# Attention followed by a gated linear unit: the depthwise convolutions of two units on one full TensorE array, with a new order of work

## The chip, the cores and the metric

One core of one Trainium2 chip. The metric is the device time of a run in microseconds (us); profile spans, given beside it, run from the first to the last instruction of one profiled execution.

## The reference, cut to what matters

B = 8 batches, H = 12 heads, S = 448 positions, D = 64, model width 768, convolution width K = 5.

```python
scores = q @ k.T / sqrt(D);  scores = where(causal, scores, -1e9)   # per head
x = softmax(scores) @ v                  # heads put side by side: [B, S, 768]
gate = sigmoid(causal depthwise convolution of x along S, with conv_w[K, 768])
out = (gate * (x @ w_val)) @ w_out       # float32
```

## The kernel before

The work is cut into 24 **units**: unit `n` is batch `n // 3` and a group of four heads. Each unit has scores in two stages, exps on ScalarE, causal masks on GpSimd, attention, a normalization on VectorE and a convolution. A batch has three value products (`val`), and each pair of batches 14 output blocks (`project`). The casting DMAs (q, k, both weight matrices), the masks and the casts of v to bf16 are all written on GpSimd, which works through them in program order. v itself is loaded by SyncE.

The convolution multiplies with 32x32 diagonal matrices, so each matmul takes one tile of the array. One unit has eight tiles per tap:

```python
def conv(n):
    x = xs[n % 8]; g = n % NG
    for t in range(KW):
        for dh in range(2):
            for i in range(G):
                j = 2 * (i % 2) + dh
                r = slice(32 * i, 32 * (i + 1))
                nc.tensor.matmul(
                    out=av_ps[i // 2][32 * j:32 * (j + 1), 0:S], lhsT=cwd[r, 2 * g + dh, t], rhs=x[r, dh, t:t + S],
                    start=t == 0, stop=t == KW - 1, skip_group_check=True, tile_position=(32 * i, 32 * j))
    ...   # two tanh on ScalarE
```

The loop takes one unit at a time:

```python
for n in range(N + 1):
    load_v(n + 2)
    ...
    scores(n, 0); softmax_numerators(n, 0)          # exps, then masks
    ...                                             # n == 0: value weights
    attend(n - 1); normalize(n - 1)                 # denominators, attention product
    next_out(limit, z_ps); next_out(limit, den_ps)  # two output blocks, in some units three
    scores(n, 1); softmax_numerators(n, 1)
    conv(n - 1)
    transposes(n + 1)
    cast_v(n + 1)                                   # a unit ahead of its use
    load_qk(n + 3)
    ...                                             # val(b - 1, g, (den_ps, z_ps))
```

The softmax here doesn't subtract the row's maximum and nothing guards it: scores larger than these inputs give would overflow.

## Time and profile before

| | before |
|---|---|
| median of 4 runs | 239.17 us (237.81 to 241.24) |
| profile span | 238.6 us |
| TensorE busy | 211.0 us, 88% |
| mean granted clock | 0.986 |

The prediction below shows the stretches and the timeline. These are the rows of the profile's 40 slices of the span for the kernel before (each 6 us; tenths busy, and tenths of the full TensorE clock). In all lines of the profile PE is TensorE, PEld its weight loads, DVE VectorE, ACT ScalarE and POOL GpSimd; L12 is line 12 of the kernel, and a bracket gives the idle time before an instruction and what ended it:

```profile
PE   0297389988988999999999999999999999999893
PEclk9999859999999999999999999999999999999999
```

After the seventh slice TensorE is nearly full and its clock reads full. Before it there are holes, and the clock row dips in two slices.

### The profile page before, as it was taken

The page shows a single profiled execution, that of the slowest core. Times are in us where ns is not written, and L with a number is a line of the kernel's source. Part 1 is how long each engine was busy: PE and PEld are TensorE (multiplying, and loading weights), DVE is VectorE, ACT ScalarE, POOL GpSimd, SP SyncE. Part 2 cuts the span into 40 slices and gives each one's busy share as a digit, 9 for nine tenths or more (in the row PEclk, how much of TensorE's full clock was granted, in tenths as well). Part 3 has the DMA queues.
Part 4 walks back from the last instruction along what each step waited for, and adds up shares of the span by engine and source line. Part 5 has one row for each costly group of instructions (what it writes and reads, how often), then busy time and mean ns, then how long its engine had stood idle before and what let it go on. Part 6 is the DMA issues. An engine that isn't in the chain of part 4 may idle for free.

```text
span 238.6 us, 10214 instructions
## 1 busy us (share of the span) xinstructions
PE 211.0 (88%) x4518; PEld 117.1 (49%) x4518; DVE 138.1 (58%) x235; ACT 143.1 (60%) x201; POOL 110.7 (46%) x189
## 2 busy tenths in 40 slices
PE   0297389988988999999999999999999999999893
PEld 0154145554544555545554555555555555544462
DVE  3457466754776678657766776586678663622100
ACT  2367543488765677668676867776777677231241
POOL 7594795153746535733655365347534532100000
PEclk9999859999999999999999999999999999999999
DMA  6999999959795568787768876877797111111153
GB/s 124 225 192 161 191 217 206 176 145 213 152 203 111 103 147 163 156 189 166 145 152 209 180 121 162 235 154 155 184 191 140 41 69 69 69 65 70 69 201 132
DMA packets 59574, 36.07 MB, mean 151 GB/s; under 512 B 48261, under 2 KB 55941, under 8 KB 59530
## 3 DMA queue, kind: packets, MB, share of 16 engines
q0 software_dynamic: 10944, 13.38, 35.4%
q1 hardware_dynamic: 48586, 22.04, 35.0%
q8 instruction: 35, 0.57, 1.0%
q14 instruction: 9, 0.07, 0.1%
HBM read 37.76 MB, written 11.01 MB: 204 GB/s over the span
## 4 chain that ended last, share of the span: by engine, by line
PE 77%; DMA 9%; POOL 3%; DVE 3%; issue 3%; ACT 3%; SPq 0%; POOLq 0%; DVEq 0%
PE den_ps L230 11%; PE z_ps L230 10%; PE av_ps L214 9%; PE z_ps L248 9%; PE sc_ps L154 9%; PE av_ps L187 8%; DMA kb<-in_k_dram 7%; PE den_ps L248 7%; PE sc_ps L248 5%; PE den_ps L187 5%; PE av_ps L230 2%; ACT ob L250 2%; ACT pt L163 1%; DMA vf<-in_v_dram 1%; DVE x L200 1%
## 5 line engine op out<-in xcount | busy, mean ns | idle before, releaser
L163 ACT ACTIVATE pt<-sc_ps 128x1024 bf16<-128x1024 f32 x96 | 93.0, 1021 | 50.4 <-PE sc_ps L154 49.1
L173 POOL TENSOR_SCALAR_AFFINE_SELECT pt<-pt 128x512 bf16<-128x512 bf16 x48 | 29.6, 642 | 59.3 <-ACT pt L163 48.4
L154 PE MATMUL sc_ps<-qt,kt 32*128 32x448 bf16 (+3 forms) x768 | 35.0, 285 | 17.7 <-DVE kt L140 13.4
L248 PEld LDWEIGHTS <-gv 128*32 128x32 bf16 x1344 | 35.3, 97 | 20.1 <-issue 5.3
L230 PEld LDWEIGHTS <-wv 128*128 128x128 bf16 x288 | 26.4, 98 | 30.4 <-issue 8.1
L154 PEld LDWEIGHTS <-kt 32*128 32x128 bf16 x768 | 17.4, 96 | 41.9 <-DVE kt L140 14.7
L232 DVE SCALAR_TENSOR_TENSOR gv<-gate,den_ps 128x448 bf16<-128x448 f32 x22 | 13.7, 621 | 32.5 <-ACT gate L219 22.6
L214 PE MATMUL av_ps<-x,cwd 32*32 32x448 bf16 x960 | 29.8, 349 | 2.3 <-DVE x L200 2.2
L200 DVE TENSOR_TENSOR x<-av_ps,rb 128x448 bf16<-128x448 f32 x48 | 27.7, 620 | 3.1
L230 PE MATMUL den_ps<-x,wv 128*128 128x448 bf16 x132 | 28.8, 354 | 0.0
L230 PE MATMUL z_ps<-x,wv 128*128 128x448 bf16 x132 | 28.6, 352 | 0.0
L76 POOL CAST vb<-vf 128x1024 bf16<-128x1024 f32 x24 | 24.9, 1037 | 6.7 <-DMA vf<-in_v_dram 6.7
L248 PE MATMUL z_ps<-wo,gv 128*32 128x384 bf16 x576 | 27.6, 326 | 0.0
L167 POOL TENSOR_SCALAR_AFFINE_SELECT pt<-pt 128x512 bf16<-128x512 bf16 x24 | 15.4, 642 | 25.6 <-ACT pt L163 25.6
L194 DVE STREAM_TRANSPOSE dt<-den_ps 128x448 f32<-128x448 f32 x24 | 15.6, 650 | 19.9 <-PE den_ps L187 19.9
L140 DVE STREAM_TRANSPOSE qt<-qb 128x448 uint32<-128x448 uint32 x24 | 22.9, 952 | 7.0 <-DMA qb<-in_q_dram 7.0
L187 PE MATMUL av_ps<-pt,vb 128*32 128x448 bf16 (+3 forms) x768 | 26.7, 283 | 0.0
L219 ACT ACTIVATE gate<-av_ps 128x448 f32<-128x448 f32 x48 | 23.7, 555 | 1.1 <-PE av_ps L214 0.8
L140 DVE STREAM_TRANSPOSE kt<-kb 128x448 uint32<-128x448 uint32 x24 | 22.4, 934 | 2.5 <-DMA kb<-in_k_dram 2.5
L248 PE MATMUL den_ps<-wo,gv 128*32 128x384 bf16 x456 | 21.9, 326 | 0.0
L187 PEld LDWEIGHTS <-vb 128*32 128x32 bf16 x768 | 17.2, 101 | 6.0 <-issue 0.8
L250 ACT ACTIVATE ob<-z_ps 128x384 f32<-128x384 f32 x24 | 11.8, 491 | 13.3 <-PE z_ps L248 13.3
(36 smaller groups left out, 161.7 us busy)
## 6 DMA issues: line engine op xcount, KB each, us to landing
out_dram<-ob SPq DMA_DIRECT2D x28, 384.0 KB, 3.4
vf<-in_v_dram SPq DMA_DIRECT2D x72, 128.0 KB, 4.5
qb<-in_q_dram POOLq DMA_DIRECT2D x24, 224.0 KB, 3.9
kb<-in_k_dram POOLq DMA_DIRECT2D x24, 224.0 KB, 5.1
vf<-in_v_dram SPq DMA_DIRECT2D x24, 64.0 KB, 3.7
wv<-in_moe_w_val_dram POOLq DMA_DIRECT2D x6, 192.0 KB, 10.6
wo<-in_moe_w_out_dram POOLq DMA_DIRECT2D x6, 192.0 KB, 8.2
cwn<-in_moe_conv_w_dram SPq DMA_DIRECT2D x1, 15.0 KB
```

What stands on the lines that cost most here:

```text
L76: nc.gpsimd.tensor_copy(out=t, in_=vfs.pop(n))
L140: nc.vector.transpose(out=t.bitcast(U32).rearrange("p (b s) -> p s b", s=T), in_=qks.pop((name, n)).rearrange("p s d -> p (s d)").bitcast( ...
L154: nc.tensor.matmul(out=sc_ps[h // 2][:, h % 2, c0:c0 + nq], lhsT=kt[r, e, k0:k0 + 128], rhs=qt[r, e, q0:S], start=e == 0, stop=e == 1, ski ...
L163: nc.scalar.activation(out=pt[:, 2 * hp:2 * hp + 2, 512 * stage:512 * (stage + 1)], in_=sc_ps[hp], func=AF.Exp, scale=D ** -0.5)
L173: nc.gpsimd.affine_select(out=pt[:, :, c:c + 128], in_=pt[:, :, c:c + 128], compare_op=ALU.is_ge, fill=0.0, base=0, pattern=[[0, G], [1, 1 ...
L187: nc.tensor.matmul(out=o, lhsT=w, rhs=pt[:, h, col:col + nq], start=i == 0, stop=i == 3, skip_group_check=True, tile_position=(0, 32 * h))
L200: nc.vector.tensor_tensor(out=x[:, dh, 4:S + 4], in0=av_ps[dh][:, 0:S], in1=r, op=ALU.mult)
L214: nc.tensor.matmul(out=av_ps[i // 2][32 * j:32 * (j + 1), 0:S], lhsT=cwd[r, 2 * g + dh, t], rhs=x[r, dh, t:t + S], start=t == 0, stop=t == ...
L219: nc.scalar.activation(out=gate[:, e], in_=av_ps[e][:, 0:S], func=AF.Tanh, scale=0.5)
L230: nc.tensor.matmul(out=o[e][:, 0:S], lhsT=wv_sb[c][:, f:f + 128], rhs=xs[(NG * b + cg) % 8][:, ce, 4:S + 4], start=c == 0, stop=c == NE - ...
L248: nc.tensor.matmul(out=o[r, 0:384], lhsT=gvs[p][g][:, dh, 128 * m + 32 * j:128 * m + 32 * (j + 1)], rhs=wo_sb[c][:, f], start=c == 0, stop ...
L250: nc.scalar.activation(out=ob[:, f], in_=o[:, 0:384], func=AF.Copy, scale=0.5)
```

## The change

The intent is to have two units share the array. Their eight tiles each become sixteen, with the heads of one unit swapped in pairs so that its tiles fall where the other's do not. The convolution moves to the four score banks, the loop takes units in pairs, the start is written out by hand, and ten idle matmuls at the very beginning are to keep the clock up. A head swap needs its own copies of the value weights and of the convolution tiles, four versions instead of three.

```diff
-    def conv(n):
+    def conv(p, banks):
+        units = (2 * p, 2 * p + 1)
         for t in range(KW):
             for dh in range(2):
                 for i in range(G):
+                    for u, n in enumerate(units):
+                        j = 2 * ((i ^ swapped(n)) % 2) + dh
...
+    def prefetch(n):
+        transposes(n + 1)
+        cast_v(n)
+        load_qk(n + 4)
... the start, from unit 1's first scores (cut at both ends)
+    exps(1, 0, 2)
+    conv_tiles()
+    attend(0)
+    normalize(0)
+    load_v(3)
+    exps(1, 1, 2)
+    load_wv(1, 0)
+    load_wv(1, 1)
+    cast_v(1)
+    transposes(2)
+    exps(2, 0, 2)
+    load_wv(2, 0)
+    load_wv(2, 1)
+    attend(1)
...
+    for p in range(2, N // 2 + 1):
+        n = 2 * p
+        load_v(n + 1)
+        exps(n, 0)
+        attend(n - 1)
+        normalize(n - 1)
+        next_outs(1, [z_ps])
+        exps(n, 1)
+        next_val((den_ps, z_ps))
+        prefetch(n)
+        conv(p - 1, sc_banks)
+        next_val(av_ps)
         if n < N:
+            load_v(n + 2)
+            exps(n + 1, 0)
+            attend(n)
+            normalize(n)
+            next_outs(1, [z_ps])
+            exps(n + 1, 1)
+            prefetch(n + 1)
+            next_outs((3, 3, 2)[p % 3], (den_ps, z_ps))
+            if p == 2:
+                for c in range(NE):
+                    load_wo(c)
```

`exps` is the scores, exps and masks of one stage; its last argument splits the scores by heads. `load_wv(i, half)` issues two DMAs.

## The prediction

> **What bounds the kernel now.** I read the page's sums and slices first, then the busy time by stretches, then the timeline of one unit (one batch of four heads; there are 24 units), then the waits of the first 60 us.
>
> The stretches show where TensorE has no time left. Columns: stretch, its length, busy time of each engine, granted clock, DMA share, GB/s.
>
> ```profile
> 0.00:8.60 8.60, 0.00 (x1) 0.01 (x2) 3.10 (x17) 1.28 (x1) 4.66 (x16) 1.00 0.85 162
> 8.60:31.00 22.40, 14.29 (x282) 7.70 (x286) 12.97 (x20) 13.59 (x16) 17.59 (x29) 0.94 1.25 187
> 31.00:43.00 12.00, 11.83 (x153) 6.12 (x146) 7.11 (x12) 4.75 (x6) 7.82 (x13) 0.84 1.14 209
> ...
> 107.00:131.00 24.00, 24.00 (x556) 13.27 (x548) 16.97 (x28) 17.20 (x24) 12.82 (x22) 1.00 0.76 167
> ```
>
> From 83 to 203 us every stretch reads PE 24.00 of 24.00: TensorE is the bound there, and a microsecond taken out of its order of work is a microsecond of time, unless a wait replaces it. Before 31 us it is busy for 14.3 of 31 us, with DMA saturated.
>
> One unit in the steady part, TensorE alone (start, length to the modelled end, operation, count):
>
> ```profile
> 114.39 0.63 PE L154 MATMUL sc_ps<-qt,kt 32*128 32x448 bf16 x16
> 114.95 0.62 PE L187 MATMUL den_ps<-pt,ones 128*32 128x448 bf16 x16
> 115.40 1.05 PE L187 MATMUL av_ps<-pt,vb 128*32 128x448 bf16 x32
> 116.27 1.15 PE L248 MATMUL z_ps<-wo,gv 128*32 128x384 bf16 x24
> 117.25 1.15 PE L248 MATMUL den_ps<-wo,gv 128*32 128x384 bf16 x24
> 118.33 0.64 PE L154 MATMUL sc_ps<-qt,kt 32*128 32x320 bf16 x16
> 118.90 1.14 PE L214 MATMUL av_ps<-x,cwd 32*32 32x448 bf16 x40
> 119.97 1.31 PE L230 MATMUL den_ps<-x,wv 128*128 128x448 bf16 x6
> 121.11 1.30 PE L230 MATMUL z_ps<-x,wv 128*128 128x448 bf16 x6
> 122.35 0.63 PE L154 MATMUL sc_ps<-qt,kt 32*128 32x448 bf16 x16
> ```
>
> Lengths overlap, so I take differences of starts: scores 0.56 and 0.57, denominators 0.45, attention 0.87, two output blocks 2.06, convolution 1.07, value product 2.38; together 7.96 us. A batch (three units) has seven output blocks, 24.84 us by the chain's repeat (98.69 to 123.53), so **two units cost 16.56 us** on average.
>
> The first 60 us (who waits for whom, us in total, times, longest):
>
> ```profile
> ACT pt L163 <- PE sc_ps L154: 23.6, 8, 7.6
> PEld L154 <- DVE kt L140: 14.7, 4, 8.6
> ```
>
> TensorE waits for transposed k at 8.60 and again until 30.68: unit 3's k, issued at 17.69 behind six value-weight loads, was transposed only at 29.68.
>
> **What the Trainium skill says.** (1) TensorE: Matmul & The Clock Gate, "Part 3: Packing small matmuls — row/col tiling": 16 tiles of 32x32 run together, the span being one matmul plus about 4 ns per further tile; 10.6x was measured for 16 tiles. The trace agrees for eight: the convolution's 40 matmuls start over 1.14 - 0.35 = 0.79 us, that is four steps of 0.19 (448 columns at 2.4 GHz are 0.187) and eight starts within 0.03. (2) TensorEngine Tiling (Array Packing), "Key Properties": changing the tiling mode drains the array. Convolution 1.07 against 5 x 0.19 = 0.95 leaves 0.12 for that. (3) PSUM — Partial Sum Buffer, "PSUM bank collisions raise a hardware error": two row tiles must not write one bank and quadrant together. This is why two units can share the array only with heads swapped in one: each row tile then feeds four different column tiles, the units having banks of their own. No run shows a collision. (4) ScalarE: Activation LUTs, "What ACT_TABLE_LOAD costs": 186 ns + 0.833 ns per element. The trace agrees: 1021 ns for 1024 columns (1039 computed), 555 for 448 (559).
>
> **The change, part by part.**
>
> *Convolution of two units.* 80 matmuls per pair still in five rounds: 5 x 0.19 + 16 x 0.004 + 0.12 = 1.13 us in place of 2.14. Gain 1.0 us per pair, 12 pairs: **12 us**.
>
> *Banks and tanh.* The convolution moves to the score banks. ScalarE evicts with two tanh of 896 columns (186 + 0.833 x 896 = 932 ns, an estimate from that skill page) for four of 555. Fits: the exps of the last scores take 1.94 us after 0.2 and lie beside the first value product (2.38); both tanh take about 1.8 and lie beside the second. No TensorE wait.
>
> *New order.* An even unit now has one output block between its two score stages, the odd unit one there and two or three after its second. I laid ScalarE beside TensorE, from the end of the odd unit's second scores. Exps end at 2.14. With three blocks on two banks, the third needs the first's eviction, which runs after the exps and ends near 2.65; TensorE arrives at 2.05: 0.6 us wait. With two blocks, the next unit's scores and denominators come at 2.7, but GpSimd's masks (0.63 each, after the exps) end at 3.6, while the unmasked chunks carry TensorE only to 3.0: 0.6 us wait. So **0.6 us per pair** comes back, and a pair becomes 16.56 - 2.14 + 1.13 + 0.6 = 16.15 us. The wait that goes the other way: convolution no longer follows a fresh normalization, which cost TensorE 2.2 us in all and up to 0.3 per unit between 59 and 83 us.
>
> *Start.* v is held back behind q's first transpose, q and k of units 1 to 3 go ahead of the value weights, and ten idle matmuls keep the clock up. First scores: VectorE now makes convolution weights (a dozen small copies, about 2 us estimated from the 516 ns of the old, larger ones) before its transposes, so I expect 8.1, not 8.6. Then ScalarE bounds: eight exp pairs x 1.94 + 2 us of tanh, to about 27 us. But the data of units 0 to 4, v to unit 3 and three of four value-weight versions are 2.30 + 1.84 + 1.18 = 5.3 MB (0.459 MB per unit and tensor pair as counted at the destination); at the 190 GB/s of the early stretches that is 28 us after 2.5. So the pair loop starts near **30 us**. The kernel before is at the same work at 43.7 less three value products (7.1) and one convolution (1.1): 35.5. Gain 5.5 us. The next two pairs stay DMA-bound (the fourth weight version adds 0.39 MB; up to 3 us wait), but the kernel before also waits between 43 and 83 us (3.7 us idle of 40), so I leave the gain at 5.5.
>
> *End.* Still three value products and some fourteen output blocks after the last convolution, with the same waits of 0.59 us for an eviction of the same tile: gain under 1 us.
>
> Sum: 238.6 - 12 (convolution) - 5.5 (start) - 0.7 (end) + 0.6 x 10 pairs (new waits) = 226.4 in the profile. The timed median, 239.99, is 1.4 us above the profile's span, and the lowest run below it; I take **226.5 us**.
>
> **The rivals.**
> (a) *TensorE cannot be fed fast enough.* A pair is 160 instructions (each matmul has its weight load) in 1.1 us, 7 ns each; over a unit of the kernel before 360 instructions go in 7.96 us, 22 ns each, and by the starts in the trace its densest 48 matmuls still need about 1.2 us. Nothing shows a sustained rate as high. If instructions cost 15 ns beyond a full queue of 64, a pair takes some 1.5 us, and 4.5 us of the gain go: 231. For it: nothing in the profile, only absence of proof; against it: pairs of weight load and matmul start 3.3 ns apart within a round, from a filled queue.
> (b) *The new order costs more than 0.6 us per pair,* since outputs come in one lump behind the exps, and score banks now serve scores, convolution and the end. If 1.3 us per pair: 234. For it: ScalarE is in order and has 11.7 us of work per 16. Against: ACT is only at 60%.
> (c) *No new waits, start better than DMA allows on average* (share 1.14 to 1.25 at up to 209 GB/s): 12 + 8 gone and nothing back, 219.
> (d) *DMA keeps the start as it was*: gain 12 - 6 only, 233.
>
> **Range and chances.** Slower needs (a), (b) and (d) together and more; the convolution's saving alone is 5% of the time, and even half of it is over 2%. I put the range at 218 to 234 and the chances at 0.90 faster, 0.08 same, 0.02 slower.
>
> **What would show it.** Convolution rows: 80 matmuls of 448 columns in about 1.1 us, 12 times; over 1.4 means (a). Steady pairs of 16.1 us for 4.67 output blocks, TensorE idle about 0.6 in each, its releaser the eviction of an output block or the mask; 24.00 of 24.00 again with a pair of 15.6 would be (c). First scores near 8.1 and unit 4's scores near 30 us; 26 or less, or 35, would make the start wrong. The granted clock should stay near 1.00 in the stretch 31 to 43, where it was 0.84. The prediction fails if the convolution's rounds step by more than 0.19 us, or if the loop's idle time exceeds 1.3 us per pair.

## The result, and the profile after

| | before | after |
|---|---|---|
| median | 239.17 us (4 runs) | 248.15 us (4 runs, 247.6 to 249.62) |
| ratio, 95% interval | | 1.0377 (1.0283 to 1.0472): slower |
| profile span | 238.6 us | 245.8 us |
| mean clock | 0.986 | 0.949 |

A ratio here is the mean time of one kernel's fast runs over that of the kernel before in the same rounds, so not quite the ratio of the medians quoted. The kernel before had medians of 239.17 to 239.89 us.

The same two rows of the page, after:

```profile
PE   7783853996989999998999999989999999888892
PEclk9998677796899999999999999999999999999998
```

TensorE now starts at once, but the clock is at 0.6 to 0.8 in six of the seven slices from the fifth to the eleventh (24.6 to 67.6 us); the kernel before was below 0.9 in two slices only (24 to 36 us).

**How the clock is read here.** In the first 20 us the clock row can't be trusted: it reads 0.9 there, and the matmuls are slow. These are the first five idle matmuls and the first scores of the kernel after:

```profile
1.26 2.31 PE L131 MATMUL z_ps<-idle 128*128 128x512 bf16 x5 [1.26 <-DVE eye L116]
...
7.14 1.06 PE L178 MATMUL sc_ps<-qt,kt 32*128 32x448 bf16 x16
```

Five such idle matmuls take 1.24 us in a late gap of run e13 (below), and such scores 0.63 in the steady loop. So I go by durations: scores of 0.63 us and an attention product of 1.05 mean the full clock, about 1.05 and 1.90 the **half clock**. By them the ten idle matmuls did not bring the clock up: it was half until about 20 us (18 in the kernel before). It also means that the clock given for a whole run, or for a stretch that begins before some 25 us, can be too high, and differs between runs with the same durations: from 16.0 to 25.3 us e1 reads 1.00 and e5 0.50, with second attention products of 1.71 and 1.91 us.

**Where the time went.** I laid the two kernels side by side by the start of each unit's first scores. Units 4, 8 and 22 are good marks:

| first scores of | before | after |
|---|---|---|
| unit 4 | 43.68 | 37.83 |
| unit 8 | 73.98 | 77.13 |
| unit 22 | 186.94 | 193.23 |
| end of the span | 238.6 | 245.8 |

A mark is not equal work. At unit 8 the kernel after has still to do one unit's convolution (1.07), one value product (2.38) and two output blocks (1.96) that the kernel before has done, 5.4 us at the kernel before's prices. So it is 3.15 + 5.4 = **8.6 us behind** there. From unit 8 to unit 22 it takes 116.1 against 112.96 us, and does five output blocks more (33 against 28, 4.9 us): 1.8 better. About that much is what the kernel before loses in its unit 8 alone, which has no output blocks to fill with (7.63 us from 73.98 to 81.61, where the prediction's parts without blocks add to 5.90). Against the kernel before's steady price the loop is **level**: 16.57 us per pair (mean of its three kinds, 16.70, 16.66 and 16.36, each from one odd unit's first scores to the next) and 16.56. In the end it loses 0.4. In all: 8.6 - 1.8 + 0.4 = 7.2, the difference of the spans.

The loop did get its convolutions cheaper. This is TensorE around one of them (start, us to the modelled end, operation, count, idle time before and its releaser):

```profile
149.56 1.25 PE L239 MATMUL sc_ps<-x,cwd 32*32 32x448 bf16 x80
150.74 2.44 PE L262 MATMUL av_ps<-x,wv 128*128 128x448 bf16 x12
```

From start to start 1.18 us for 80 matmuls, against 2 x 1.07 before. So the loop, level as a whole, loses elsewhere what it gains there, and the start loses much more. The waits of the whole kernel after name the candidates (us in total, times, longest):

```profile
PE av_ps L212 <- POOL vb L86: 10.0, 7, 2.8
PE den_ps L281 <- ACT ob L283: 2.1, 6, 0.3
PE sc_ps L178 <- DVE kt L162: 5.5, 5, 2.4
```

The first, the attention product waiting for v's cast on GpSimd, is on none of my lists. The chain of waits of the kernel after (start, us, what), from one cast in the start to the next, shows how it comes about:

```profile
14.88 1.05 POOL vb L86
...
15.97 1.90 PE av_ps L212 x16
17.87 0.98 PE sc_ps L178 x15
...
18.87 1.95 ACT pt L187 x2
...
20.88 1.22 POOL pt L197 x2
...
22.58 1.58 POOL wv L95 x3
24.16 1.05 POOL vb L86
```

Read it downwards. The cast lets the attention product run, the second scores stand behind that on TensorE, their exps behind the scores, their masks behind the exps, and then GpSimd's own order puts four value-weight issues (2.11 us in the timeline) between the masks and the **next** unit's cast; in the two rounds after this one it is two and four issues of q and k. The cast needs nothing from the masks; its v had landed. But it is written behind them, so one serial chain, 9.3 us long here, passes through four engines for each unit. The attention products start at 15.97, 25.26, 33.58 and 42.95: periods of 9.3, 8.3 and 9.4 us, where ScalarE is busy for 3.9 to 5.4 us and GpSimd, the busiest engine there, for 6.3 to 7.6 (the next view; its issues of DMAs count).

The stretches show what TensorE does in those periods (stretch, length, busy time of PE, PEld, DVE, ACT and POOL, clock, DMA share, GB/s):

```profile
16.00:25.30 9.30, 4.89 (x84) 2.51 (x88) 5.16 (x9) 3.88 (x4) 7.44 (x14) 0.86 1.31 200
25.30:33.60 8.30, 6.13 (x164) 3.60 (x167) 4.21 (x7) 5.43 (x8) 6.25 (x11) 0.71 0.96 147
33.60:43.00 9.40, 4.75 (x84) 2.34 (x88) 4.63 (x8) 3.96 (x5) 7.60 (x14) 0.68 0.97 168
58.00:69.00 11.00, 11.00 (x188) 5.45 (x184) 6.21 (x10) 5.60 (x6) 9.99 (x18) 0.74 0.81 147
```

TensorE is busy half to three quarters of the time, the clock falls to 0.68, and the attention product then takes 1.90 us instead of 1.05 and the second scores 0.98 instead of 0.57: the idleness lengthens the chain that made it. Even from 58 to 69 us, with TensorE busy throughout, the clock is only 0.74. DMA is at its share of the start before only in the first of these stretches.

In the first two pairs of the loop (units 4 to 7) two more waits follow. In the odd half of the first there is no output block yet to fill with, and TensorE waits for the next unit's transposed k (behind the normalization on VectorE). In the second pair it waits for the output weights, which were issued only from 60.66 us on; the last of them landed at 72.67:

```profile
57.84 1.04 PE L178 MATMUL sc_ps<-qt,kt 32*128 32x448 bf16 x16 [2.40 <-DVE kt L162]
...
72.72 0.35 PE L281 MATMUL z_ps<-wo,gv 128*32 128x384 bf16 x4 [0.60 <-DMA wo<-in_moe_w_out_dram]
```

In the steady loop, a pair with three blocks in its lump has a wait before the third, for the eviction of the first from the same bank, and 0.15 before the denominators:

```profile
142.42 1.16 PE L281 MATMUL den_ps<-wo,gv 128*32 128x384 bf16 x24 [0.35 <-ACT ob L283]
143.51 0.64 PE L178 MATMUL sc_ps<-qt,kt 32*128 32x448 bf16 x16
```

By starts the third block comes 1.49 after the second (140.93 to 142.42), where 0.98 is the price: 0.51. A pair with two blocks waits for the cast of v, again written behind the masks:

```profile
158.94 0.63 PE L178 MATMUL sc_ps<-qt,kt 32*128 32x448 bf16 x16 [0.17 <-DVE kt L162]
159.51 0.82 PE L212 MATMUL den_ps<-pt,ones 128*32 128x448 bf16 x16
161.01 1.06 PE L212 MATMUL av_ps<-pt,vb 128*32 128x448 bf16 x32 [0.69 <-POOL vb L86]
```

The attention product starts 1.50 after the denominators instead of 0.45, so 1.05, and 0.23 goes before the scores for k. That makes 0.66, 0.66 and 1.28 for the three kinds of pair, **0.87 on average**. (The page gives less for each in its brackets, because it counts idle time against modelled ends.)

### The profile page after: what moved, and what is told of

Same layout as the page of the kernel before. It is cut to its first block, busy times and chain, and to the rows that moved or that the text cites. A ratio compares the mean times of both kernels' runs of the same rounds, so it can differ in the third digit from the quotient of the medians.

```text
span 245.8 us, 10137 instructions
## 1 busy us (share of the span) xinstructions
PE 214.1 (87%) x4530; PEld 117.7 (48%) x4530; DVE 139.7 (57%) x247; ACT 140.5 (57%) x179; POOL 116.1 (47%) x199
## 4 chain that ended last, share of the span: by engine, by line
PE 58%; issue 11%; DMA 10%; POOL 9%; ACT 8%; SPq 1%; POOLq 1%; DVE 0%; ACTq 0%
PE av_ps L262 10%; PE av_ps L212 8%; PE sc_ps L178 7%; PE z_ps L281 6%; PE den_ps L262 6%; ACT pt L187 6%; PE z_ps L262 5%; PE sc_ps L239 5%; DMA vf<-in_v_dram 5%; PE sc_ps L281 4%; DMA wo<-in_moe_w_out_dram 4%; POOL vb L86 3%; PE den_ps L212 3%; ACT ob L283 3%; PE den_ps L281 2%
## 5 line engine op out<-in xcount | busy, mean ns | idle before, releaser
L281 PEld LDWEIGHTS <-gv 128*32 128x32 bf16 x1344 | 34.5, 97 | 25.3 <-issue 11.7
L178 PE MATMUL sc_ps<-qt,kt 32*128 32x64 bf16 (+3 forms) x768 | 37.6, 297 | 7.5 <-DVE kt L162 5.5
L212 PE MATMUL av_ps<-pt,vb 128*32 128x448 bf16 (+3 forms) x768 | 29.4, 303 | 10.0 <-POOL vb L86 10.0
L281 PE MATMUL z_ps<-wo,gv 128*32 128x384 bf16 x672 | 32.5, 326 | 0.7 <-DMA wo<-in_moe_w_out_dram 0.6
L246 ACT ACTIVATE gate<-sc_ps 128x896 f32<-128x896 f32 x22 | 19.0, 914 | 20.1 <-PE sc_ps L239 20.1
L262 PE MATMUL av_ps<-x,wv 128*128 128x448 bf16 x144 | 29.3, 353 | 0.0
L283 ACT ACTIVATE ob<-z_ps 128x384 f32<-128x384 f32 x28 | 13.9, 497 | 14.8 <-PE z_ps L281 13.7
L265 DVE SCALAR_TENSOR_TENSOR gv<-gate,av_ps 128x448 bf16<-128x448 f32 x24 | 14.9, 621 | 12.2 <-PE av_ps L262 11.6
L281 PE MATMUL den_ps<-wo,gv 128*32 128x384 bf16 x384 | 18.5, 327 | 2.1 <-ACT ob L283 2.1
L212 PE MATMUL den_ps<-pt,ones 128*32 128x448 bf16 (+3 forms) x384 | 17.3, 288 | 2.4 <-POOL pt L197 1.0
L262 PE MATMUL den_ps<-x,wv 128*128 128x448 bf16 x72 | 16.6, 370 | 0.0
```

Source lines behind the costliest of these rows:

```text
L178: nc.tensor.matmul(out=sc_ps[h // 2][:, h % 2, c0:c0 + nq], lhsT=kt[r, e, k0:k0 + 128], rhs=qt[r, e, q0:S], start=e == 0, stop=e == 1, ski ...
L212: nc.tensor.matmul(out=o, lhsT=w, rhs=pt[:, h, col:col + nq], start=i == 0, stop=i == 3, skip_group_check=True, tile_position=(0, 32 * i_out))
L246: nc.scalar.activation(out=gates[n], in_=sc_ps[u][:, :, 0:S], func=AF.Tanh, scale=0.5)
L262: nc.tensor.matmul(out=o[e][:, 0:S], lhsT=wv_sb[version(NG * b + cg)][:, ce, f:f + 128], rhs=xs[(NG * b + cg) % 8][:, ce, 4:S + 4], start= ...
L281: nc.tensor.matmul(out=o[r, 0:384], lhsT=gvs[p][g][:, dh, 128 * m + 32 * j:128 * m + 32 * (j + 1)], rhs=wo_sb[c][:, f], start=c == 0, stop ...
L283: nc.scalar.activation(out=ob[:, f], in_=o[:, 0:384], func=AF.Copy, scale=0.5)
```

## The experiments

**Theory (A where an expectation uses a letter).** The packing works, and the order of work as written on the in-order engines costs more than it gives: in the start GpSimd's weight issues and masks ahead of casts that could go earlier, with the clock falling in the gaps; in the loop the same cast, and one bank too few for the lump of output blocks. **Rivals.** The start is bound by the bytes (the fourth weight version adds some); the packed convolution gives less than its rows suggest; the clock alone does it. Each edit is against the kernel after unless said otherwise. All results were correct.

| run | median us | ratio to before, 95% | span | clock |
|---|---|---|---|---|
| after | 248.15 | 1.0377 (1.0283 to 1.0472) | 245.8 | 0.949 |
| e1_start_cast | 243.15 | 1.0159 (1.0107 to 1.0212) | 241.2 | 0.975 |
| e2_loop_cast | 244.95 | 1.0253 (1.0184 to 1.0322) | 243.7 | 0.947 |
| e3_conv_apart | 252.11 | 1.0530 (1.0478 to 1.0582) | 251.1 | 0.969 |
| e4_third_bank | 245.45 | 1.0239 (1.0186 to 1.0293) | 244.9 | 0.965 |
| e5_qk4_first | 241.15 | 1.0076 (1.0014 to 1.0138) | 241.1 | 0.949 |
| e6_p2_early | 240.22 | 1.0019 (0.9962 to 1.0075) | 238.6 | 0.964 |
| e8_all_mended | 231.35 | 0.9666 (0.9615 to 0.9718) | 229.5 | 0.983 |
| e9_all_swap | 234.21 | 0.9782 (0.9724 to 0.9840) | 232.3 | 0.990 |
| e10_keep_warm | 247.09 | 1.0334 (1.0278 to 1.0389) | 246.6 | 0.975 |
| e11_mended_apart | 236.80 | 0.9902 (0.9863 to 0.9941) | 234.9 | 0.985 |
| e12_mended_v_free | 233.99 | 0.9782 (0.9740 to 0.9825) | 231.7 | 0.982 |
| e13_mended_warm | 230.72 | 0.9659 (0.9610 to 0.9708) | 227.7 | 1.000 |
| e14_loop_only | 241.38 | 1.0058 (1.0012 to 1.0105) | 239.5 | 0.963 |
| e15_warm_short | 244.03 | 1.0171 (1.0126 to 1.0216) | 241.9 | 0.986 |
| e16_tail_banks | 227.80 | 0.9475 (0.9416 to 0.9534) | 227.9 | 0.993 |

(The profile of e16 fell on the slowest of its runs, and so did that of e5.) Differences of 2 to 3 us between two of these kernels stand only just clear of the spread of their runs; those of under 1 us (e6 against e5, e13 against e8) do not.

### e1_start_cast: the casts of units 1 to 3 ahead of masks and weight issues

```diff
     load_v(3)
+    cast_v(1)
     exps(1, 1, 2)
     load_wv(1, 0)
     load_wv(1, 1)
-    cast_v(1)
     ...            # likewise cast_v(2) and cast_v(3)
```

> In the start alone, the casts of v for units 1, 2 and 3 go ahead of the second masks and of the value-weight issues in GpSimd's order. Theory A (GpSimd's order made a serial loop of 8.3 to 9.4 us per unit in the start): a loop now lacks the weight issues (2.1 us) and the cast (1.05), so about 3 us per unit, three units: 6 to 9 us less than the changed kernel, 239 to 242 us, and unit 4's scores near 30 us in place of 37.8 (those of unit 8 near 69 in place of 77). Rival B (the start is bound by data: v held back, more weight bytes): the casts then wait for v, and the time stays within 2 us of 248.

Measured: 5.0 us less than after, with the same bytes and the same work. TensorE in the start:

```profile
22.93 1.71 PE L212 MATMUL av_ps<-pt,vb 128*32 128x448 bf16 x32
...
36.43 1.04 PE L178 MATMUL sc_ps<-qt,kt 32*128 32x448 bf16 x16 [4.73 <-DVE kt L162]
```

The second attention product starts at 22.93 instead of 25.26 with no wait before it, and unit 8's first scores at 72.51 instead of 77.13. So the order, not the volume of DMA, made these 5 us. But unit 4 came only 1.4 us earlier: a new wait took the chain's place, for unit 4's k: GpSimd issues that unit's q and k loads at 29.65, behind weight issues, masks and a cast.

### e5_qk4_first and e6_p2_early: the next two waits of the start

e5 is e1 with the loads of unit 4's q and k ahead of all value weights. e6 is e5 with two changes in the pairs: the transposes for the next even unit ahead of the normalization, and the output weights issued half a pair earlier.

```diff
     transposes(1)
+    load_qk(4)               # e5 and e6
     load_wv(0, 0)
...
             exps(n + 1, 0)
+            transposes(n + 2)  # e6; no longer in prefetch(n + 1)
             attend(n)
...
         prefetch(n)
+        if p == 2:             # e6; moved up from the odd half
+            for c in range(NE):
+                load_wo(c)
         conv(p - 1, sc_banks)
```

> The run with the casts moved in the start, and q and k of unit 4 issued ahead of the value weights. In that run TensorE waited 4.73 us for unit 4's transposed k, whose load was issued at 29.65 behind twelve weight issues. Theory A (GpSimd's order, now the order of issues): unit 4's scores come near 32.5 in place of 36.4 and the time falls by 2 to 4 us against that run, to 240. Rival B (data bound): the weights come later by as much, and the first value product waits for them instead: within 1 us of 243.

> As the run before, and in the pair loop the next even unit is transposed ahead of the normalization, and the output weights are issued half a pair earlier. Theory: the first two pairs lose 2.4 us to the transposes and 1.5 us to the output weights, with the clock halved after it: 3 to 5 us less than the run before, 236. Rival B: the output weights only push q and k back, under 1.5 us less.

Measured: e5 241.15, another 2.0 less than e1, with unit 4 at 34.64. Bytes and work are the same again; two issues moved forward in GpSimd's program. (The intervals of e1 and e5 overlap, and the profile of e5, its slowest run, has unit 8 at 72.03 against 72.51.) e6 gave only 0.9 more, within the spread of the runs, where I expected far more (240.22 instead of 236). In its profile unit 8 starts at 69.88: the wait of 2.40 for unit 6's k is gone, but TensorE waits 1.04 and 0.54 us in its place for exps on ScalarE. Its seven pairs to unit 22 still take 116.1 us, as in after. The start is now worth 7.9 us of the kernel after, and the loop has not moved.

### e2_loop_cast, e4_third_bank and e14_loop_only: the loop's waits, singly and together

```diff
     def prefetch(n):
         transposes(n + 1)
-        cast_v(n)
+        cast_v(n + 1)          # e2 and e14, with load_v one unit earlier too
...
-            next_outs((3, 3, 2)[p % 3], (den_ps, z_ps))
+            next_outs((3, 3, 2)[p % 3], (den_ps, z_ps, av_ps[0]))   # e4 and e14
```

> In the pair loop alone, v is cast one unit earlier, so that the cast lies ahead of the masks (loads of v one unit earlier too). Theory C (new waits of the loop eat the gain of the packed convolution): the 0.69 us wait of the attention product for the cast goes from the pairs with two output blocks, and 1 to 2 us from the first two pairs: 2 to 4 us less, 244 to 246; the two-block pair takes 15.9 in place of 16.36 us. Rival: the masks end at the same time and TensorE waits for them instead, no change over 1 us.

> The third output block of a pair goes to the free attention bank in place of the denominator bank. Theory C: the waits of 0.51 and 0.15 us for evictions go in the seven pairs with three blocks: 3.5 to 4.5 us less, 244 us; such a pair takes 16.1 in place of 16.70 us. Rival: ScalarE is behind anyway (exps, then evictions) and the wait moves to the next scores or attention product: under 1.5 us less.

> The changed kernel with both mends of the loop (earlier cast, third bank) and its start as it was. Alone they gave 3.2 and 2.7 us. If each only removes its own wait: 5.9 together, 242.3. If the third bank alone moved TensorE's wait on to the cast (its attention product after three blocks then waited for it), both together free what one could not: 7 to 9 us, 240.

Measured: -3.2, -2.7, and together -6.8 (241.38, between my two expectations). TensorE in e4, after three blocks:

```profile
143.04 0.62 PE L212 MATMUL den_ps<-pt,ones 128*32 128x448 bf16 x16
143.80 1.06 PE L212 MATMUL av_ps<-pt,vb 128*32 128x448 bf16 x32
```

The third block no longer waits, but the attention product now comes 0.76 after the denominators instead of 0.45: part of the wait had moved on to the cast. So the two edits do more together than apart. In the medians the difference is small (6.8 against 5.9), but from unit 8 to unit 22, where after takes 116.1 us, e2 gains 1.6 us (114.5), e4 0.9 (115.2) and both 4.9. In e14 the seven pairs there take 111.2 us, 15.88 each instead of 16.59 (116.1 / 7): the two waits were what kept the loop from its gain, and without them it is under the 16.15 that I had predicted.

### e3_conv_apart and e11_mended_apart: everything but the packing

The loop over units goes outermost in `conv`, so each pair runs two eight-tile convolutions one after the other, in the same place and banks. e3 is on after, e11 on e8 (below).

```diff
-        for t in range(KW):
-            for dh in range(2):
-                for i in range(G):
-                    for u, n in enumerate(units):
+        for u, n in enumerate(units):
+            for t in range(KW):
+                for dh in range(2):
+                    for i in range(G):
```

> The two convolutions of a pair one after the other, eight tiles each, all else as in the changed kernel. If the packing is a true gain on the path: ten rounds of 0.19 in place of five, 0.95 us per pair, 12 pairs: 259 us. If the packed convolution's gain is lost in waits anyway (the tanh, the score banks): under 252.

> The kernel with all waits mended (231.35), with the two convolutions of a pair one after the other. In the changed kernel this took 1.70 in place of 1.17 us per pair and 4 us in all, since the second unit's first round runs beside the first unit's last (nine rounds, not ten). On the path here too: 0.53 x 12 = 6 us more, 236 to 238. If the mended loop has slack there: under 2 us more.

Measured: e3 252.11, so +4.0 where I expected 259 (and just over the 252 under which I would have called the gain lost); e11 236.80, so +5.5, as expected. TensorE in e3:

```profile
152.33 1.76 PE L239 MATMUL sc_ps<-x,cwd 32*32 32x448 bf16 x80
154.03 2.44 PE L262 MATMUL av_ps<-x,wv 128*128 128x448 bf16 x12
```

Apart, the pair takes 1.70 us from start to start, not 2.14. A round is a set of tiles that start together. The trace has eight rounds in each pair, not ten (nor the nine of my expectation for e11): 8, 8, 8, 16, 16, 8, 8 and 8 matmuls, 0.19 us apart. So in two of them tiles of the second unit start beside tiles of the first (the two units use different tiles). What is over of the 0.44 us saved, some 0.06, fits one change of mode in place of two, which no run isolates. Of the 0.96 us that a pair gained, 0.44 thus came from putting two units one behind the other and 0.53 from interleaving their tiles. Over twelve pairs the interleaving is 6.4 us by these rows and was timed at 4.0 in the kernel after, and 5.5 in the mended one. The rest of e3 against before, +12.5 us, is what the change costs without the interleaving, though with the 0.44 us per pair.

### e10_keep_warm and e15_warm_short: is the half clock itself on the path?

Idle matmuls (128x128 by 512 columns) between the denominators and the attention product of units 1 to 3, twelve in e10 and five in e15.

```diff
         for dh in (2, 0, 1):
+            if dh == 0 and n in (1, 2, 3):
+                keep_clock(12)        # e15: 5
```

> The changed kernel with twelve idle matmuls (2.6 us at full clock) ahead of the attention product of units 1, 2 and 3, where TensorE waits 1.5 to 2.8 us for the cast of v. If the half clock of that stretch (0.68 to 0.71) is on the path: attention 1.05 in place of 1.90 and scores 0.63 in place of 1.04, three units and the first value product: 3 to 4 us less, 244.5. If the loop of GpSimd's order alone sets it and the clock only follows: within 1.5 us of 248, or slower by what the fill overlaps.

> Five idle matmuls in place of twelve ahead of the attention product of units 1 to 3 of the changed kernel: 2.2 us at half clock, which fits in the waits of units 1 and 3 (2.8) where twelve overran them. If the half clock is on the path of the start: unit 4's scores 2 us earlier than 37.8 and the time 2 to 3 us less, 245.5. If GpSimd's order alone sets it: within 1 us of 248.

e10 settled nothing: its filling ran from 22.41 to past 26.7, where the wait for the cast would have ended at 25.26, so it delayed what it was to speed up (247.09). e15's ended in time and gave -4.1 us. The second attention product of after:

```profile
25.26 1.90 PE L212 MATMUL av_ps<-pt,vb 128*32 128x448 bf16 x32 [2.81 <-POOL vb L86]
```

The same one in e15:

```profile
24.71 1.06 PE L214 MATMUL av_ps<-pt,vb 128*32 128x448 bf16 x32 [0.70 <-POOL vb L86]
```

The attention products of units 1 to 3 take 1.06, 1.06 and 1.15 us instead of 1.90 each, and the second scores behind them about 0.65 instead of 1.05; GpSimd's order is the same. Unit 4 comes at 36.37 instead of 37.83 and unit 8 at 73.15 instead of 77.13. So the half clock is on the path of the start in after: it is a cause of its own, though one that the waits bring about.

### e8_all_mended: all amends together, and three variants of it

e8 is e6 with the edits of e2 and e4 as well.

> All of these moves with the earlier cast in the loop and the third bank for output blocks. If the parts add up: 248 less 5 (casts in the start), 3 (order of issues), 4 (transposes, output weights), 3 (loop cast), 2.7 (third bank): near 231, below the kernel before by 3 to 4%. If they hide one another (one wait put in the place of another): 236 to 240.

Measured: 231.35, as expected from adding up: 16.8 less than after, 8.5 less than before in the same rounds. Unit 8's first scores start at 66.43, and the seven pairs from there to unit 22 take 111.7 us. So the change **with** its convolution packing pays, once the waits are out of the way.

e12 is e8 without the hold-back of v behind q's transpose (`transposes(0)` instead of `transposes(0, v_f[0])`); e13 is e8 with unit 4's transposes earlier and six idle matmuls in each of two gaps; e9 is e8 with the second value product and the lump of output blocks exchanged.

> The mended kernel without the write that holds v back behind q's first transpose. If holding v back helps (q and k of unit 0 land sooner): first scores about 1 us later and 0.5 to 1.5 us more, 232.5. If v is what the start lacks (its first cast keeps TensorE waiting 0.58 us): up to 1 us less.

> The mended kernel with unit 4's transposes ahead of unit 2's normalization, and six idle matmuls in each of the two remaining gaps (before the scores of units 4 and 6), after which the clock is halved. If transposes and clock are what is left in the start: 2.1 us wait becomes about 1, and 3 us of half clock go: 228 to 229. If ScalarE's exps bound it there: within 1 us of 231.

> As the last, but the second value product of a pair changes places with the lump of output blocks: the blocks stand behind the convolution (two tanh, 1.7 us, to hide) and the product behind the odd unit's second scores (exps and masks, 3.4 us, to hide). If the loop's remaining waits are those for exps and masks, a pair takes 15.6 in place of about 16.0 us and the time is 2 to 4 us below the last run. If the evictions behind the tanh wait instead, the same or slower.

e12: +2.6 us, the first scores at 8.77 instead of 7.34; the hold-back, which my prediction mentions, earns its place. e13: full clock from about 23 us on (e8 falls to the half clock twice after that), and a median within 1 us of e8's. It changes two things at once, and its profile, on its fastest run, has unit 8 at 64.23 instead of 66.43. So once the chain of casts is cut the two together are worth little, and the clock's own share isn't shown. e9 missed: its pairs are faster (110.3 us from unit 8 to 22 against 111.7), but with the lump ahead of the value product that makes blocks available, three more blocks fall to the end, and it is 2.9 us slower.

### e16_tail_banks: a better version

The end of e13 has TensorE waiting for the eviction of a block from the same tile of PSUM, though the other bank of that tile was free; the first of five such lines:

```profile
202.58 1.16 PE L281 MATMUL sc_ps<-wo,gv 128*32 128x384 bf16 x24 [0.64 <-ACT ob L283]
```

e16 lets neighbouring blocks take different tiles (against e13):

```diff
-    next_outs(2, sc_banks[0])
+    next_outs(2, [sc_banks[0][0], sc_banks[1][0]])
     next_val((den_ps, z_ps))
-    next_outs(2, sc_banks[1])
+    next_outs(2, [sc_banks[0][1], sc_banks[1][1]])
     next_val(av_ps)
-    next_outs(len(outs), [*sc_banks[0], *sc_banks[1], *av_ps, den_ps, z_ps])
+    next_outs(len(outs), [sc_banks[0][0], sc_banks[1][0], den_ps, sc_banks[0][1], sc_banks[1][1], z_ps, *av_ps])
```

> The mended kernel with the fill (230.72), with the output blocks after the loop alternating between tiles of PSUM, so that no block waits 0.59 to 0.64 us for the eviction of the block before it. Five such waits: 3 us less, 227.5. If ScalarE's evictions bound the end instead: under 1 us less.

```profile
205.07 2.13 PE L281 MATMUL sc_ps<-wo,gv 128*32 128x384 bf16 x48
```

Two blocks now run through without a gap. 227.80 us, 2.9 less than e13 and 5% less than before (ratio 0.9475): the fastest kernel.

## Why the prediction was wrong, point by point

The profile span was to be 226.4 and is 245.8. The 19.4 us fall into three terms, each read off at the marks above. The prediction's figures put unit 4's first scores at 30 us, and unit 8's at 73.98 - 5.4 (less work done) - 7.3 (5.5 of the start, 3 convolution pairs at 1.0, 1.2 of waits back) = 61.3 us.

- **Start, to unit 4: 7.8 us of the miss (37.83 instead of 30).** The step that failed reads "Then ScalarE bounds". It took the start as the larger of ScalarE's time and the DMA's, and never wrote out GpSimd's program, in which a cast stands behind masks and two to four issues. Each of three units then took 8.3 to 9.4 us, so the serial chain bound the start of after, and not ScalarE or the bytes. e1 shows this by moving the casts alone (5.0 us), e5 by moving two issues; e15 shows the share of the clock. Up to unit 4 itself the record does not close: it starts at 36.43 in e1, 34.64 in e5 and 32.51 in e13, where the transposes and the clock are mended too. The last 2.5 us to the predicted 30 stay open. The estimate from DMA volume may hold there: DMA is as busy in these starts as in the start before (share 1.21 to 1.27 in e8 from 16.0 to 33.6 us), and no run takes bytes away.
- **First two pairs, to unit 8: 8.0 us of the miss** (39.3 us from unit 4 to unit 8 instead of 31.3). The prediction said "up to 3 us wait" and left it out. Named waits of 2.78 for a cast, 2.40 for k and 0.60 for the output weights stand there, and the half clock accounts for the rest (two attention products at 1.90 instead of 1.05, with scores and value products about them). The prediction expected the clock to "stay near 1.00" for the ten idle matmuls at the beginning; that step failed too. They ran at the half clock themselves, and so did the work behind them until about 20 us; then the waits brought the half clock back.
- **Loop and end: 3.6 us of the miss.** "0.6 us per pair comes back" was right in kind and too small: 0.87. For the three-block pair the releaser was named rightly and the size too (0.66). For the two-block pair the step looked at the masks alone, while the cast of v stands behind them on the same engine: 1.28. The pairs took 16.57 us instead of 16.15; 0.27 of that is waits and 0.05 the convolution. I did not follow the last 0.10 further.
- **Convolution: right.** 80 matmuls in 1.18 us, against 1.13 predicted (1.75 in the first of the twelve pairs, at the half clock); the rival that TensorE can't be fed is dead. The prediction's reason was half right, for interleaving earns 0.53 per pair, and putting one unit behind the other the other 0.44.
- **First scores: right in direction** (7.14 instead of 8.1 predicted and 8.6 before). **Tanh: right**: 914 ns, estimated 932.
- **The rivals.** (b), the order costs more than expected, was the nearest; it was looked for in the loop at 1.3 us per pair, and stood mostly in the start. (d), DMA keeps the start as it was, fell with e1, for the start of after. The chances were too bold: I wrote that "slower" needs three rivals together, where one unlisted chain in the start was enough to eat the gain.

The gain went, then, in this order: the start turned it into a serial chain (7.9 us back with e6), the loop into new waits (6.8 us back with e14). e8 recovers 16.8, more than 7.9 + 6.8. By the profiles the surplus lies before unit 8: it comes 10.7 us earlier than in after in e8, 7.3 in e6 and 0.1 in e14, while from unit 8 to unit 22 e8 gains no more than e14 (4.4 and 4.9 us). e6 has more half clock there (0.80 and 0.64 in the two stretches from 25.3 to 43.0 us, where e8 reads 1.00 and 0.82), but no run isolates that.

## What to carry to other kernels

When a new order of work is written, lay out the program of **every** in-order engine through the start, and count the busy time by stretches: GpSimd, at under half busy over the whole run, was the busiest engine of the start (75 to 81% of its stretches) and set the pace, because a cast that needed nothing stood behind masks that needed the whole round of the other engines. Move work that is ready early ahead of work that waits, and keep it a unit ahead in the loop. When a packing is priced, compare with the same work put back to back, since part of the gain may come from that alone. And check by the durations whether idle matmuls bring the clock up at all.

## What the Trainium skill lacked or had wrong

- TensorE: Matmul & The Clock Gate, "Part 3: Packing small matmuls — row/col tiling": its model for sixteen tiles held (five rounds, 1.18 us for 80 matmuls). It gives no figure for two eight-tile groups on different tiles, issued one after the other: they overlap in two of their rounds already, 1.70 us where two separate groups take 2.14, so interleaving gains 0.53 and not 1.0.
- The same page, "HAM oscillation — how this bites in real kernels", gives "no PE-idle gaps >~3.4µs" as the rule; only a kernel with much shorter idling between groups is told of after it, with no number for how much idling it takes. Here idle waits of at most 2.81 us, with TensorE busy for 51 to 74% of a stretch, went with a clock of 0.68 to 0.71 from 25.3 to 43.0 us, and the attention product at 1.90 us instead of 1.05. Five idle matmuls in each of three such waits brought it to 1.06 to 1.15 and took 4.1 us off the kernel.
- DMA: Bandwidth & Descriptors, "Issuing engines are not separate DMA queues", calls the time to initiate a DMA "usually small relative to the DMA itself". That section does not say what it does to the issuing engine's other work: an issue took GpSimd 0.53 to 0.57 us in the start of after, and four of them held a cast, and with it TensorE, for 2.1 us.
